# Transposing the last 64 keys of a mixed attention tile: one fp32 matmul with 128 weight columns from a zero-padded tile, in place of two with 64

## The chip, the cores and the metric

The kernel runs on one core of a Trainium2 chip, in one launch. The metric is device time in microseconds (us). A core has TensorE (PE in the profile, with its weight loads as PEld), VectorE (DVE), ScalarE (ACT), GpSimd (POOL) and SyncE (SP, which issues most DMAs). Each engine works through its own list in order and waits on semaphores where it needs another's result.

## What is computed

Four batches of 576 tokens go through attention with 8 heads of 64, then a gated expert layer, then a Fourier mixing layer with an MLP. The change lies in the attention, which keeps only scores close to each row's largest:

```python
scores = scale * np.matmul(q, k.transpose(0, 1, 3, 2))
thresh = np.max(scores, axis=-1, keepdims=True) - tau
scores = np.where(scores >= thresh, scores, -1000000000.0)
scores = scores - np.max(scores, axis=-1, keepdims=True)
attn = np.exp(scores)
attn = attn / (np.sum(attn, axis=-1, keepdims=True) + 1e-09)
return np.matmul(attn, v)
```

Behind it stand two matrix products with a squared ReLU between them and a sigmoid gate (the expert layer), and then the two Fourier transforms, a normalisation and two more products (the mixer).

## The kernel before, in words

**Tiles.** The 32 heads are worked on as 16 pairs (`pi`), two heads (`j` = 0, 1) each. A head has 576 = 4 x 128 + 64 query rows, so a pair has eight tiles of 128 rows that belong to one head, and a ninth, the *mixed* tile, with the last 64 rows of head 0 on partitions 0 to 63 and those of head 1 on partitions 64 to 127. The nine are the steps of a pair, the mixed one the fifth. Step `n` of the whole program is `9 * pi + s`.

**One step.** PE makes the scores of a tile from a query tile and the keys, which are split into a high and a low part (`kh`, `kl`) so that two fast matmuls give fp32 accuracy (L212, and L226 for the mixed tile). DVE takes the row maximum (L252), ACT the exponential (L263), DVE drops what lies below the threshold and sums (L267), takes the reciprocal (L626, L630), and `emit_norm` multiplies the tile by it (L273 on POOL; in the first four pairs most tiles on ACT, L636). The tile `e` is then transposed on PE, 128 keys at a time, since the product with V needs keys on partitions. ACT and DVE split each transpose into a high and a low part (L305, L306). Eight or so of these feed `emit_av` (L387, L389).

**The last 64 keys.** 576 keys are four blocks of 128 and 64 more. A head's own tiles get the 64 along with 64 of the other head (L340). In the mixed tile both heads' last 64 keys stand in columns 512 to 575, on different partitions, and the product with V wants head 0's keys on partitions 0 to 63 and head 1's on 64 to 127. `emit_Tmix` therefore ends, in `out2`, with two matmuls (L365): weights are all 128 rows and 64 columns of `e`, the moving operand is a set of 32 identity columns that picks one head's half, and each writes one half of the partitions of `t2`:

```python
for j in range(2):
    c = 64 * j + 32 * half
    pe.matmul(t2[64 * j:64 * j + 64], e[:, 512:576], ident[:, c:c + 32], start=True, stop=True)
```

They are fp32 and not transposes. `emit_Tmix` runs twice for each pair (`half` = 0, 1), so there are 32 places in the program and 64 such matmuls. Four whole transposes of the mixed tile stand ahead of each place (L353).

**Stages.** In the first four pairs only attention runs, while DVE, ACT and POOL also split the expert weights (`weight_pieces`, L54 to L73: L67 to L69 on DVE, L72 on ACT, L73 on POOL). From the fifth pair on, the expert layer of the batches that are done runs between the attention's steps (`ffn_stream`: L413 to L415, and L523 to L525, three matmuls for each product). The mixer comes last.

**What sets the order.** The program is written step by step, with a priority for each kind of work (`hp`), and a scheduler puts each engine's instructions in order from its own estimates, so an edit at one place can move rows at others. A tile of the pool `at` with one buffer (`em`, the raw head loads `raw`) is written again only when its last reader is done. A raw load is released when the splits (L151 on POOL, L167 on DVE) have read it.

Of the kernel before, what the change touches and what calls it, by code (L numbers as in the profile page):

```python
# [9 lines left out]
F32 = mybir.dt.float32  # L10
F32R = mybir.dt.float32r
I32 = mybir.dt.int32
ALU = mybir.AluOpType
AF = mybir.ActivationFunctionType
# [7 lines left out]
NPAIR = H // 2  # L22
# [6 lines left out]
def tile_kernel(ctx: ExitStack, tc: tile.TileContext, a):  # L29
    nc = tc.nc  # L30
    pe, dve, act, pool, sp = nc.tensor, nc.vector, nc.scalar, nc.gpsimd, nc.sync
# [8 lines left out]
    ident = const.tile([128, 128], F32, name="ident")  # L40
# [54 lines left out]
    at = astack.enter_context(tc.tile_pool(name="at", bufs=1, side="right"))  # L95
# [42 lines left out]
    heads, vts, ptu, ptr, et, em, sps, stat, xT = ({} for _ in range(9))  # L138
# [7 lines left out]
    def conv_k(pi, j):  # L146
        raw = heads[pi, j][0]
        kh = at.tile([128, S], F32R, tag="kh", bufs=3, name="kh")
        kl = at.tile([128, S], F32R, tag="kl", bufs=3, name="kl")
        act.activation(kh, raw[:, 640:], AF.Copy)  # L150
        (dve if pi + j == 0 else pool).tensor_tensor(kl, raw[:, 640:], kh.bitcast(F32), op=ALU.subtract)  # L151
        heads[pi, j] += [kh, kl]
# [19 lines left out]
    vtile = at.tile([128, 10, 128], F32R, name="v")  # L172
    pool.memset(vtile[:, 8:10].bitcast(F32), 0.0)

    def load_v(pi):
        b, pr = divmod(pi, NPAIR)
        raw = at.tile([128, 9, DH], F32, tag="raw", name="rawv")
        sp.dma_start(raw, a["v"][b, pr])
        vts[pi] = raw
# [14 lines left out]
    def step_of(n):  # L194
        pi, s = divmod(n, 9)
        return pi, ORDER[s]
# [34 lines left out]
    def eview(n):  # L231
        pi, tl = step_of(n)
        if tl is None:
            if n not in em:
                em[n] = at.tile([128, S], F32, tag="em", name="em")
            return em[n]
        j, i = tl
        if (pi, i) not in et:
            m = 4 * pi + i
            if P['E3'] and m % 3 == 2 and m < 4 * NPAIR - 2:  # L240
                et[pi, i] = stage.tile([128, 2 * S], F32, tag="e", name="e3")
            else:
                et[pi, i] = at.tile([128, 2 * S], F32, tag="e", bufs=2, name="e")
        return et[pi, i][:, j * S:(j + 1) * S]
# [23 lines left out]
            e, sps[n][:, :, 0:HS], st[:, 1:2], e, op0=ALU.is_ge, op1=ALU.mult, accum_out=st[:, 2:3]  # L268
        )

    def emit_norm(n):
        st, e = stat[n], eview(n)
        pool.tensor_scalar(e, e, st[:, 2:3], 1.0, op0=ALU.mult, op1=ALU.mult)  # L273

    def emit_front(n):

# [72 lines left out]
    def emit_Tmix(pi, half):  # L349
        e = em[pi * 9 + 4]  # L350
        t = pst.tile([128, 4, 2, 2, 32], F32, tag="t", name="tm")
        for k in range(4):
            pe.transpose(t[:, k].rearrange("p a b c -> p (a b c)"), e[:, 128 * k:128 * (k + 1)], ident)  # L353
        sl = slice(256, HS)

        def out():
            for j in range(2):
                u = unit(pi, j, half)
                split_out(u[:, 0, :, sl], u[:, 1, :, sl], t[:, :, j, half, :])

        def out2():
            t2 = pst.tile([128, 32], F32, tag="t", name="tm2")
            for j in range(2):
                c = 64 * j + 32 * half
                pe.matmul(t2[64 * j:64 * j + 64], e[:, 512:576], ident[:, c:c + 32], start=True, stop=True)  # L365
            r = rem_unit(pi, half)
            split_out(r[:, 0, sl], r[:, 1, sl], t2)

        return [out, out2]
# [200 lines left out]
    sp.dma_start(mus[:, 0:4], a["mu_k"])  # L570
    sp.dma_start(mus[:, 4:8], a["mu_r"])
    dve.tensor_scalar(mus[:, 8:16], mus[:, 0:8], -1.0, 1.0, op0=ALU.mult, op1=ALU.add)
    conv_k(0, 1)
    conv_q(0, 1)
    load_v(0)
    conv_v(0)

# [31 lines left out]
    def do_front(n, pi, s):  # L609
        cur = 0 <= n < NSTEP  # L610
        nxt = range(state['m'], min(n + ahead(n), NSTEP - 1) + 1)
        state['m'] = max(state['m'], n + ahead(n) + 1)
        k = 1
        if s != 4 and P['SM' if pi >= NPAIR else 'SM0'] >> ((s - (s > 4)) // 2) & 1:

            k = 0 if s in (0, 2, 5, 7) else 2
        g = stats.rearrange("p (s c) -> p s c", c=3)[:, s + 1 - k:s + 1]
        with hp('pF'):
            if cur:
                emit_select(n)  # L620
        with hp('pM'):
            for m in nxt:
                emit_max(m)
        with hp('pF'):
            if cur and k:
                dve.tensor_scalar(g[:, :, 2], g[:, :, 2], 1e-9, None, op0=ALU.add)  # L626
            for m in nxt:
                emit_th(m)
            if cur and k:
                dve.reciprocal(g[:, :, 2], g[:, :, 2])  # L630
        with hp('pN'):
            for m in range(n + 1 - k, n + 1):
                if cur:
                    if P['NA' if pi >= NPAIR else 'NA0'] >> (m % 9) & 1:
                        e = eview(m)
                        act.activation(e, e, AF.Copy, scale=stat[m][:, 2:3])  # L636
                    else:
                        emit_norm(m)

    def do_av(n, pi, s):  # L640
        for d in range(2):
# [74 lines left out]
    for n in range(NSTEP + 8):  # L716
        pi, s = divmod(n, 9)
# [347 lines left out]
    for (q, g), f in mixer():  # L1065
# [4 lines left out]
        if f == 2 and (q, g) in ahead_of:  # L1070
            while (q, g) == (0, 5) and not fft_done:
                next(behind)
            n = ahead_of[q, g]
# [134 lines left out]
```

## Time and profile before

| what | value |
|---|---|
| median of 3 runs | 1136.56 us (1135.72 to 1139.6) |
| the profiled execution | 1139.89 us, of which 1138.1 us is the span of the trace |
| busy, share of the span | PE 91%, PEld 84%, DVE 71%, ACT 52%, POOL 43% |
| mean granted TensorE clock | 0.969 of full speed |
| instructions | 19981, on PE 7109 matmuls |
| DMA | 114.07 MB, mean 100 GB/s |

The busy shares are means over stages with different limits, so the rows further down are taken stage by stage. A matmul's end in the profile is modelled; its start is not, so PE is read by the distance between starts. In a form like `128*64 128x32` the first is the weights' rows and columns and the second the moving operand's.

### The profile page before, as it was taken

The page shows a single profiled execution, that of the slowest core. Times are in us where ns is not written, and L with a number is a line of the kernel's source. Part 1 is how long each engine was busy: PE and PEld are TensorE (multiplying, and loading weights), DVE is VectorE, ACT ScalarE, POOL GpSimd, SP SyncE. Part 2 cuts the span into 40 slices and gives each one's busy share as a digit, 9 for nine tenths or more (in the row PEclk, how much of TensorE's full clock was granted, in tenths as well). Part 3 has the DMA queues.
Part 4 walks back from the last instruction along what each step waited for, and adds up shares of the span by engine and source line. Part 5 has one row for each costly group of instructions (what it writes and reads, how often), then busy time and mean ns, then how long its engine had stood idle before and what let it go on. Part 6 is the DMA issues. An engine that isn't in the chain of part 4 may idle for free.

```text
span 1138.1 us, 19981 instructions
## 1 busy us (share of the span) xinstructions
PE 1038.4 (91%) x7109; PEld 960.0 (84%) x7109; DVE 806.7 (71%) x2093; ACT 588.9 (52%) x1396; POOL 483.8 (43%) x633
## 2 busy tenths in 40 slices
PE   4566769999999999999999997999999999999998
PEld 3555649999988999889988986889999999999997
DVE  7999889889889798897865677975553959322222
ACT  5787777768586685866736564433331212111111
POOL 4556576746467364673634253530001636100000
PEclk9888789999999999999999998999999999999999
DMA  5333321101112011121016255663442546223231
GB/s 171 111 119 96 98 73 56 48 30 54 55 56 76 30 47 56 56 76 32 24 65 159 93 162 178 199 205 120 153 143 90 185 158 190 98 93 109 77 111 56
DMA packets 40395, 114.07 MB, mean 100 GB/s; under 512 B 6191, under 2 KB 6612, under 8 KB 40296
## 3 DMA queue, kind: packets, MB, share of 16 engines
q1 hardware_dynamic: 27200, 74.57, 20.4%
q0 software_dynamic: 10400, 33.50, 9.1%
q10 hardware_dynamic: 2696, 4.73, 1.2%
q8 instruction: 56, 0.92, 0.3%
q14 instruction: 43, 0.35, 0.1%
HBM read 84.45 MB, written 28.32 MB: 99 GB/s over the span
## 4 chain that ended last, share of the span: by engine, by line
PE 65%; DVE 16%; ACT 7%; DMA 6%; issue 4%; POOL 2%; SPq 0%; DVEq 0%; ACTq 0%; POOLq 0%
PE c1ps L969 6%; PE c1ps L971 6%; PE c1ps L970 6%; PE c2ps L984 6%; PE c2ps L982 6%; PE c2ps L983 6%; PE av L387 3%; PE s L212 3%; DVE q L167 3%; DMA rawqk<-in_qk 2%; PE t L320 2%; DVE small L252 2%; PE kps L413 2%; DVE e L267 2%; PE kps L415 2%
## 5 line engine op out<-in xcount | busy, mean ns | idle before, releaser
L975 DVE SCALAR_TENSOR_TENSOR hl<-c1ps,hh 128x256 fp32r<-128x256 f32 x144 | 60.4, 421 | 161.2 <-ACT hh L974 160.6
L974 ACT ACTIVATE hh<-c1ps 128x256 fp32r<-128x256 f32 x144 | 54.3, 379 | 205.7 <-PE c1ps L971 205.6
L252 DVE TENSOR_REDUCE small<-s 128x1 f32<-128x576 f32 x144 | 107.3, 750 | 15.7 <-PE s L212 14.7
L1007 POOL DMA_DIRECT2D ud<-u x54 | 29.5, 546 | 194.2 <-DVE u L1006 138.4
L267 DVE SCALAR_TENSOR_TENSOR e<-s,small,e 128x576 f32<-128x576 f32 x128 | 102.4, 811 | 7.3 <-ACT e L263 5.6
L273 POOL TENSOR_SCALAR e<-e,small 128x576 f32<-128x576 f32 x104 | 82.3, 797 | 46.4 <-DVE small L630 35.4
L263 ACT ACTIVATE e<-s,small 128x576 f32<-128x576 f32 x128 | 92.6, 742 | 14.4 <-DVE small L252 13.4
L212 PE MATMUL s<-kh,q 128*128 128x288 f32 x256 | 65.4, 340 | 29.8 <-DVE q L167 13.7
L320 PE MATMUL t<-ident,e 128*128 128x128 f32 x512 | 81.2, 290 | 7.9 <-DVE ptr L306 2.9
L969 PE MATMUL c1ps<-ut,cA 128*128 128x256 f32 x288 | 82.5, 286 | 2.2 <-ACT ut L960 1.5
L970 PE MATMUL c1ps<-ut,cA 128*128 128x256 f32 x288 | 82.0, 285 | 0.0
L523 PE MATMUL vps<-k,wv 128*128 128x288 f32 x256 | 76.7, 302 | 5.4 <-DVE tg L529 4.6
L971 PE MATMUL c1ps<-ut,cA 128*128 128x256 f32 x288 | 81.6, 283 | 0.0
L971 PE MATMUL c1ps<-ut,cB 128*128 128x256 f32 x288 | 81.0, 281 | 0.0
L969 PE MATMUL c1ps<-ut,cB 128*128 128x256 f32 x288 | 80.9, 281 | 0.0
L970 PE MATMUL c1ps<-ut,cB 128*128 128x256 f32 x288 | 80.7, 280 | 0.0
L485 POOL TENSOR_TENSOR k<-relu,k 128x288 fp32r<-128x288 f32 x64 | 54.1, 847 | 60.6 <-ACT k L483 59.7
L306 DVE TENSOR_TENSOR pt<-t,pt 128x512 fp32r<-128x512 f32 x100 | 67.8, 684 | 16.4 <-ACT pt L305 15.7
L413 PE MATMUL kps<-xh,wk 128*128 128x288 f32 x256 | 78.3, 306 | 0.8 <-ACT relu L470 0.4
L387 PE MATMUL av<-pt,v 128*128 128x288 f32 x408 | 71.3, 308 | 8.1 <-ACT pt L305 3.8
L414 PE MATMUL kps<-xl,wk 128*128 128x288 f32 x256 | 75.8, 296 | 0.0
L415 PE MATMUL kps<-xh,wk 128*128 128x288 f32 x256 | 75.6, 296 | 0.0
(240 smaller groups left out, 3552.8 us busy)
## 6 DMA issues: line engine op xcount, KB each, us to landing
rawqk<-in_qk SPq DMA_DIRECT2D x32, 608.0 KB
u<-ud SPq DMA_DIRECT2D x36, 512.0 KB
wraw<-in_w_ch POOLq DMA_DIRECT2D x64, 256.0 KB, 3.3
ud<-u POOLq DMA_DIRECT2D x54, 256.0 KB, 2.5
rawv<-in_v SPq DMA_DIRECT2D x16, 288.0 KB
un<-ud SPq DMA_DIRECT2D x18, 256.0 KB
out<-u SPq DMA_DIRECT2D x18, 256.0 KB
wraw<-in_w_k SPq DMA_DIRECT2D x8, 512.0 KB
```

The lines of the kernel that those rows point to most:

```text
L212: pe.matmul(ps[:, h, 0:HS], q[:, c:c + 128], kk[:, h * HS:(h + 1) * HS], start=(x == 0), stop=(x == 1),)
L252: dve.tensor_reduce(st[:, 0:1], sps[n][:, :, 0:HS], axis=AX.XY, op=ALU.max, negate=True)
L263: act.activation(two(eview(n)), sps[n][:, :, 0:HS], AF.Exp, bias=st[:, 0:1])
L267: dve.scalar_tensor_tensor(e, sps[n][:, :, 0:HS], st[:, 1:2], e, op0=ALU.is_ge, op1=ALU.mult, accum_out=st[:, 2:3])
L273: pool.tensor_scalar(e, e, st[:, 2:3], 1.0, op0=ALU.mult, op1=ALU.mult)
L320: pe.transpose(t[:, k, :], e[:, o + 128 * k:o + 128 * (k + 1)], ident)
L387: pe.matmul(ps, v[:, 4 * j + k, :], u[:, x, k, :], start=(k == 0 and x == 0), stop=False)
L413: pe.matmul(ps, wh, x[0][:, k, :], start=(k == 0), stop=False)
L415: pe.matmul(ps, wl, x[0][:, k, :], start=False, stop=(k == nk - 1))
L969: pe.matmul(ps, wh, ut[0][:, k, :], start=(k == 0), stop=False)
L970: pe.matmul(ps, wh, ut[1][:, k, :], start=False, stop=False)
L971: pe.matmul(ps, wl, ut[0][:, k, :], start=False, stop=(k == 3))
```

## The change

A tile `ez` of 128 x 128 is zeroed once at the start. The norm of a mixed tile is now three instructions: columns 0 to 511 in place as before, and columns 512 to 575 of each head's 64 rows into `ez`, head 0's into the upper left quarter and head 1's into the lower right one. A second tile `icomb` holds the sum of the two halves of the identity. One matmul with `ez` as weights, 128 columns wide, and 32 columns of `icomb` then gives both heads' halves at once. The choice between ACT and POOL moves into `emit_norm` and stays as it was.

```diff
--- before.py
+++ after.py
@@ -171,6 +171,11 @@
 
     vtile = at.tile([128, 10, 128], F32R, name="v")
     pool.memset(vtile[:, 8:10].bitcast(F32), 0.0)
+
+
+    ez = at.tile([128, 128], F32, name="ez")
+    pool.memset(ez, 0.0)
+    icomb = at.tile([128, 64], F32, name="icomb")
 
     def load_v(pi):
         b, pr = divmod(pi, NPAIR)
@@ -268,9 +273,19 @@
             e, sps[n][:, :, 0:HS], st[:, 1:2], e, op0=ALU.is_ge, op1=ALU.mult, accum_out=st[:, 2:3]
         )
 
-    def emit_norm(n):
+    def emit_norm(n, on_act=False):
         st, e = stat[n], eview(n)
-        pool.tensor_scalar(e, e, st[:, 2:3], 1.0, op0=ALU.mult, op1=ALU.mult)
+        parts = [(e, e, slice(0, 128))]
+        if step_of(n)[1] is None:
+            parts = [(e[:, 0:512], e[:, 0:512], slice(0, 128))]
+            for j in range(2):
+                r = slice(64 * j, 64 * j + 64)
+                parts.append((ez[r, r], e[r, 512:576], r))
+        for o, i, r in parts:
+            if on_act:
+                act.activation(o, i, AF.Copy, scale=st[r, 2:3])
+            else:
+                pool.tensor_scalar(o, i, st[r, 2:3], 1.0, op0=ALU.mult, op1=ALU.mult)
 
     def emit_front(n):
 
@@ -360,9 +375,7 @@
 
         def out2():
             t2 = pst.tile([128, 32], F32, tag="t", name="tm2")
-            for j in range(2):
-                c = 64 * j + 32 * half
-                pe.matmul(t2[64 * j:64 * j + 64], e[:, 512:576], ident[:, c:c + 32], start=True, stop=True)
+            pe.matmul(t2, ez, icomb[:, 32 * half:32 * half + 32], start=True, stop=True)
             r = rem_unit(pi, half)
             split_out(r[:, 0, sl], r[:, 1, sl], t2)
 
@@ -570,6 +583,7 @@
     sp.dma_start(mus[:, 0:4], a["mu_k"])
     sp.dma_start(mus[:, 4:8], a["mu_r"])
     dve.tensor_scalar(mus[:, 8:16], mus[:, 0:8], -1.0, 1.0, op0=ALU.mult, op1=ALU.add)
+    dve.tensor_tensor(icomb, ident[:, 0:64], ident[:, 64:128], op=ALU.add)
     conv_k(0, 1)
     conv_q(0, 1)
     load_v(0)
@@ -631,11 +645,7 @@
         with hp('pN'):
             for m in range(n + 1 - k, n + 1):
                 if cur:
-                    if P['NA' if pi >= NPAIR else 'NA0'] >> (m % 9) & 1:
-                        e = eview(m)
-                        act.activation(e, e, AF.Copy, scale=stat[m][:, 2:3])
-                    else:
-                        emit_norm(m)
+                    emit_norm(m, P['NA' if pi >= NPAIR else 'NA0'] >> (m % 9) & 1)
 
     def do_av(n, pi, s):
         for d in range(2):
```

Line numbers move by 5 to 14 in the changed kernel (L365 is L378 there, L523 to L525 are L536 to L538, L273 and L636 are L288 and L286). Three places show how the order on the engines moves.

PE, second stage, at the place that stands at 503 us in the trace of the kernel before (`vps` is the expert layer's second product, `tm` the result of the transpose). Before:

```order
L523 MATMUL vps<-k_5695,wv_86 128x288
L524 MATMUL vps<-k_5696,wv_86 128x288
L525 MATMUL vps<-k_5695,wv_87 128x288
L365 MATMUL tm_6285<-ident,em 64x32 x2
L523 MATMUL vps<-k_5695,wv_86 128x288
L524 MATMUL vps<-k_5696,wv_86 128x288
L525 MATMUL vps<-k_5695,wv_87 128x288
L212 MATMUL s<-kh,q 128x288 x2
```

With the change:

```order
L536 MATMUL vps<-k_5701,wv_86 128x288
L537 MATMUL vps<-k_5702,wv_86 128x288
L538 MATMUL vps<-k_5701,wv_87 128x288
L378 MATMUL tm_6291<-icomb,ez 128x32
L536 MATMUL vps<-k_5701,wv_86 128x288
L537 MATMUL vps<-k_5702,wv_86 128x288
L538 MATMUL vps<-k_5701,wv_87 128x288
L217 MATMUL s<-kh,q 128x288 x2
```

The neighbours are the same; two matmuls with 64 columns have become one with 128.

POOL, second stage, around the norm of the same pair's mixed tile (`kl` is the key split that releases a raw head load). Before:

```order
L189 TENSOR_TENSOR v<-rawv,v 128x4x64
L189 TENSOR_TENSOR v<-rawv,v 64x64
L273 TENSOR_SCALAR em<-em,small 128x576
L273 TENSOR_SCALAR e<-e,small 128x576
L151 TENSOR_TENSOR kl<-rawqk,kh 128x576
L441 TENSOR_TENSOR xl<-xtmp,xh 128x288 x2
L273 TENSOR_SCALAR e<-e,small 128x576
```

With the change:

```order
L194 TENSOR_TENSOR v<-rawv,v 128x4x64
L194 TENSOR_TENSOR v<-rawv,v 64x64
L288 TENSOR_SCALAR em<-em,small 128x512
L288 TENSOR_SCALAR ez<-em,small 64x64 x2
L288 TENSOR_SCALAR e<-e,small 128x576
L151 TENSOR_TENSOR kl<-rawqk,kh 128x576
L454 TENSOR_TENSOR xl<-xtmp,xh 128x288 x2
L288 TENSOR_SCALAR e<-e,small 128x576
```

The two small multiplies stand between the mixed tile's norm and the next tile's, and the key split comes behind them.

ACT, first stage, around the fourth pair's mixed tile (140 us in the trace). Before:

```order
L72 ACTIVATE wv_86<-wbits 128x512
L395 ACTIVATE xt<-avs 64x288
L188 ACTIVATE v<-rawv 64x64
L305 ACTIVATE ptr<-t_1307 128x128
L636 ACTIVATE em<-em,small 128x576
L331 ACTIVATE e<-t 128x512
L332 ACTIVATE pt<-t 128x4x128
L263 ACTIVATE e<-s,small 128x576 x2
```

With the change:

```order
L193 ACTIVATE v<-rawv 128x4x64
L320 ACTIVATE ptr<-t_1311 128x128
L193 ACTIVATE v<-rawv 64x64
L408 ACTIVATE xt<-avs 64x288
L286 ACTIVATE em<-em,small 128x512
L286 ACTIVATE ez<-em,small 64x64 x2
L408 ACTIVATE xt<-avs 64x288
L193 ACTIVATE v<-rawv 64x64
L346 ACTIVATE e<-t 128x512
```

The three norm instructions stand together; two copies of attention results (`xt`) and the parts of `v` have other places around them.

## Rows read from the trace of the kernel before

**Rows 1.** Page, part 2: granted TensorE clock in tenths, 40 slices of 28.45 us.

```profile
PEclk9888789999999999999999998999999999999999
```

**Rows 2.** Windows view, two stretches (length, then busy us and instructions by engine, clock, DMA).

```profile
0.00:184.00 184.00, 116.29 (x633) 101.86 (x634) 163.09 (x410) 134.17 (x275) 112.84 (x108) 0.84 0.35 107
184.00:590.00 406.00, 390.25 (x2982) 375.08 (x2982) 345.47 (x970) 284.62 (x676) 230.85 (x306) 1.00 0.15 47
```

**Rows 3.** Line view of L365, whole run: ns min/median/max of weight loads and matmuls.

```profile
L365 PEld LDWEIGHTS tm<-ident,em x128: 132/136/232, 41.6 to 584.7; 128*64 128x64 f32 x128
L365 PE MATMUL tm<-ident,em x128: 222/243/316, 41.6 to 584.7; 128*64 128x32 f32 x128
```

**Rows 4.** Timeline of PE matmuls, 502.9 to 504.4 us (start, length, what).

```profile
503.03 0.29 PE L525 MATMUL vps<-k,wv 128*128 128x288 f32 x1
503.25 0.31 PE L365 MATMUL tm<-ident,em 128*64 128x32 f32 x4
503.49 0.40 PE L523 MATMUL vps<-k,wv 128*128 128x288 f32 x1
503.73 0.29 PE L524 MATMUL vps<-k,wv 128*128 128x288 f32 x1
503.86 0.29 PE L525 MATMUL vps<-k,wv 128*128 128x288 f32 x1
```

**Rows 5.** Timeline of PE weight loads, same stretch.

```profile
502.90 0.19 PEld L525 LDWEIGHTS vps<-k,wv 128*128 128x128 f32 x1
503.25 0.20 PEld L365 LDWEIGHTS tm<-ident,em 128*64 128x64 f32 x4 [0.17 <-DVE small L626]
```

**Rows 6.** Timeline of PE matmuls around four full-width fp32 transposes, 582.3 to 583.3 us.

```profile
582.37 0.30 PE L525 MATMUL vps<-k,wv 128*128 128x288 f32 x1
582.50 0.60 PE L353 MATMUL tm<-ident,em 128*128 128x128 f32 x4
582.85 0.38 PE L523 MATMUL vps<-k,wv 128*128 128x288 f32 x1
583.07 0.30 PE L524 MATMUL vps<-k,wv 128*128 128x288 f32 x1
```

**Rows 7.** Timeline of PE matmuls around one with 33 rows, 623.0 to 623.9 us.

```profile
623.03 0.28 PE L817 MATMUL fa<-tc,G 128*128 128x258 f32 x1
623.24 0.38 PE L818 MATMUL fa<-talt,g 33*128 33x258 f32 x1
623.55 0.39 PE L824 MATMUL fb<-ts,H 128*128 128x256 f32 x1
```

**Rows 8.** Groups of POOL by line and shape (count, busy us, mean ns, idle before).

```profile
L437 POOL TENSOR_SCALAR xtmp<-xt,small 128x288 f32<-128x288 f32 x64 | 35.1, 554 | 28.4 <-DVE xl L441 15.3 <-DVE xt L396 12.3
...
L273 POOL TENSOR_SCALAR em<-em,small 128x576 f32<-128x576 f32 x12 | 9.0, 749 | 16.0 <-DVE small L630 9.0 <-DVE small L259 7.0
```

**Rows 9.** Groups of ACT by line and shape.

```profile
L188 ACT ACTIVATE v<-rawv 64x64 fp32r<-64x64 f32 x32 | 7.9, 248 | 0.4
...
L636 ACT ACTIVATE em<-em,small 128x576 f32<-128x576 f32 x4 | 3.1, 764 | 0.0
```

**Rows 10.** Chain of waits, 0 to 300 us (start, length, what).

```profile
2.58 3.07 DMA small<-in_mu_r
...
140.30 0.66 ACT em L636
```

**Rows 11.** Timeline of POOL, 497.5 to 500.7 us.

```profile
497.77 0.75 POOL L273 TENSOR_SCALAR em<-em,small 128x576 f32<-128x576 f32 x1 [3.52 <-DVE small L259]
...
499.21 1.43 POOL L151 TENSOR_TENSOR kl<-rawqk,kh 128x576 fp32r<-128x576 f32 x1
```

**Rows 12.** Chain of waits, 184 to 590 us.

```profile
499.65 1.69 DVE q L167
501.39 3.79 DMA rawqk<-in_qk
```

**Rows 13.** Groups of DVE by line and shape: one step of the weight conversion.

```profile
L68 DVE SCALAR_TENSOR_TENSOR wbits<-wraw,wbits 128x512 int32<-128x512 int32 x20 | 19.7, 986 | 0.1
```

## Prediction

> **What bounds the kernel now.** Read the granted clock first. In the first 184 us it moves between the two levels (1.2 and 2.4 GHz); from then on it stands at full speed but for one dip [rows 1]. The windows view shows two different stages in the part that the change touches [rows 2]. From 0 to 184 us PE is busy for 116.29 us and DVE for 163.09: DVE sets the pace, and a shorter PE step is worth little. From 184 to 590 us, where the other twelve pairs' attention runs between the matmuls of the first expert layer, PE is busy for 390.25 of 406.00 us at full clock. Its idle time is 15.75 us, 4%: work taken off PE here should shorten the stage. After 590 us no mixed tile is left, since the last L365 record starts at 584.7 us [rows 3]. Next read what one pair of L365 matmuls costs there, by start times, because the profile models the ends of matmuls.
>
> The 128 records are two passes for each of the 64 fp32 matmuls, so each of the 32 places in the program has four [rows 3]. In [rows 4], ordinary 288-column matmuls start 0.13 us apart. L525 starts at 503.03, the four records at 503.25, the next L523 at 503.49 and the one behind it at 503.73: 0.70 us, where two ordinary steps would take 0.27. **The place costs 0.43 us.** It is not computing for all of it. The loads show why: the load for L525 starts at 502.90, 0.13 us ahead of its own matmul, but the first 64-column load starts only at 503.25 [rows 5], with its own matmul and 0.22 us behind the last [rows 4]. A load that should lie under the matmul before it does not. On the way out it takes 0.24 us from one start to the next, twice.
>
> Is that fp32, or the half-width array? Two neighbours tell. Four fp32 transposes with 128 weight columns run from 582.37 to 583.07, also 0.70 us, so four cost 0.43 and one 0.11 us, with no gap around them [rows 6]. An ordinary-type matmul that uses only 33 rows at a partition offset has the gaps: 0.21 us ahead of it and 0.31 behind [rows 7], against the 0.13 of [rows 4]. So the gaps go with the part of the array, not with fp32.
>
> **The change part by part.**
>
> *PE.* Each place loses two matmuls (four loads of 64 columns) and gets one with 128 columns (two passes, two loads). No row shows a full-width fp32 matmul that is not a transpose, so I bound it. Lower: two passes at the transposes' 0.11 us, no gaps, 0.22 us [rows 6]: 0.43 - 0.22 = 0.21 us saved. Upper: the gaps stay, because the two passes of fp32 cause them. Then the two loads, one behind the other, take the place of four that overlapped. The four records last 0.31 us together and one matmul at least 0.222, so their starts lie within 0.09 us [rows 3, 4]; two loads 0.11 apart cost 0.02 more, or 0.13 more if each pass takes its whole 0.11. I take the lower end: [rows 7] has the gaps without fp32 and [rows 6] has fp32 without gaps. Of the 96 records in the stage, 24 places x 0.215 = **5.2 us less**. The eight early places count as nothing, since DVE is ahead there; at half clock each could save 0.43, 3.4 us in all, and I keep that for the lower end of the range.
>
> *POOL.* For twelve of the sixteen mixed tiles, one 576-column multiply becomes three. From 288 to 576 columns it goes from 554 to 749 ns [rows 8], 0.68 ns a column: 512 columns make 0.71 us and each 64-column one some 0.40. So 1.50 in place of 0.75: 0.75 us more, 9.0 in all, and at least nothing if the small ones were free. POOL is idle for 175 of the 406 us [rows 2]. What stands behind it matters: in [rows 11] the mixed multiply, the next tile's, and then the split of the keys into kl follow back to back. That kl ends at 500.64. The next load into the same raw buffer starts at 501.39, and in the chain it waits for DVE's q, which ends at 501.34 [rows 12]. So 0.70 us of the 0.75 is covered, and I count zero. Without that cover it is the third rival.
>
> *ACT.* Four mixed tiles are scaled on ACT: 764 ns becomes some 0.71 for 512 columns and two small ones of at least 248 ns each [rows 9], with the scale read from a tensor perhaps 0.34: +0.45 to +0.62 us. In the chain of the first stage one of the four stands [rows 10]. I count one, **0.6 us more**; none to four makes 0 to 2.5.
>
> *DVE and the start.* The sum of the two identity halves stands ahead of the 1 - mu step, for which the chain waits until 5.65 us anyhow [rows 10]: zero. If the identity landed last it would be one small operation. Zeroing ez is one memset before POOL has work: zero.
>
> *Waits.* The norm writes ez where it wrote em's last columns, and reads its place before the next pair's norm; em already had that wait, and earlier (the exponential). Nothing new is waited for. The 512-column multiply ends a little sooner, the 64-column part later, and two steps lie between them and the transposes.
>
> *The order.* The scheduler has put many things elsewhere in the first stage. The PE rows around the mixed tiles later are nearly the same. Where a weight conversion of three DVE operations of about 1 us [rows 13] comes ahead of or behind what the chain needs, a place like that is worth up to 3 us either way; I take zero.
>
> *Sum.* -5.2 on PE; a tenth of it, 0.6, is lost because the chain through q and the raw loads [rows 12] becomes last in places; +0.6 on ACT: **-4.0 us**. The profiled execution took 1139.89 us (span 1138.1 and 1.8 around it), so 1135.9 for it; the median of the runs is 1136.56, 3.3 below, so **1132.6 us**.
>
> **The rivals.**
>
> *1. The gain is taken by other waits.* PE is shortened, but the head loads and q (3.79 and 1.69 us in the chain [rows 12]) keep the pairs' rhythm. For it: they recur in the chain. Against: PE idles only 4%. Then -5.2 leaves -1 or nothing: 1135 to 1137.
>
> *2. The gaps stay.* By the upper bound 24 x 0.02 to 0.13 = 0.5 to 3.1, and 0.6 on ACT: 1137.7 to 1140.3. For it: no row has this form. Against: [rows 6, 7]. The Trainium skill speaks for it with another reason (TensorEngine Tiling (Array Packing), Key Properties): different tiles of the array can load weights and multiply in parallel, so the merge gives up a concurrency. The overlap in [rows 5], four loads in 0.20 us, agrees with that page; by it alone the sum would be this rival's.
>
> *3. POOL becomes last: slower.* At the mixed tile, kl comes late by 0.75 us, the raw buffer comes free late, and the next head's load, q and scores follow. It decides where the small multiplies cost over 0.35 us each, since the cover is 0.70 us. Wholly on the path: +9.0 - 5.2 + 0.6 = +4.4, 1141.0. For it: 0.40 is beyond 0.35. Against: q on DVE would have to end no later than now, and only 0.05 us a pair lies open.
>
> *4. The order outweighs the rest*: one or two conversions that move ahead of or behind the chain in the first stage, 3 to 6 us either way on top of the forecast: 1126.6 to 1129.6, or 1135.6 to 1138.6.
>
> **How the numbers follow.** A measurement of this kernel tells about 0.3%, 3.4 us, from no change. Forecast 60% (1127 to 1135: of these 41 are below 1133.2 and 19 within), rival 1 10% (within), rival 2 10% (7 within, 3 slower), rival 3 12% (slower), rival 4 8% (4 faster, 2 within, 2 slower). Faster 0.45, same 0.38, slower 0.17. The range goes from 1126.5 (5.2, with the early 3.4 and some luck of order) to 1140.3, the end of rival 2; beyond it lie rival 3 and the tails.
>
> **What would show it.** L365's line becomes 64 records with 128 weight columns. Right: the next ordinary matmul but one starts 0.49 us after the one ahead of the pair, not 0.70, and its first load starts with the matmul before it; the 24 places end the stage about 5 us earlier, with PE's idle time near 16 us. Wrong: a gap still ahead of that load (rival 2); PE idle time grown by about 5 us behind q (rival 1) or behind kl, with POOL's small multiplies above 0.35 us (rival 3); a first stage that is several us longer or shorter (rival 4).

## The result and the profile after

The changed kernel takes **1152.01 us** (median of 4 runs, 1149.51 to 1152.84); the kernel before, run beside it on the same chip, 1137.39. The ratio is 1.0118 with a 95% interval of 1.0101 to 1.0135: slower by 1.2%, where 1132.6 us and a gain of 0.35% were forecast. The profiled execution took 1149.51 us (span 1147.7) against 1139.89 (1138.1).

The part of the change that the argument rested on did what it was to do. The line view of L378 (the new matmul) answers to [rows 3], and the timelines of PE matmuls and weight loads at the same place of the program answer to [rows 4, 5]:

```profile
L378 PEld LDWEIGHTS tm<-icomb,ez x64: 186/190/338, 41.2 to 593.8; 128*128 128x128 f32 x64
L378 PE MATMUL tm<-icomb,ez x64: 190/275/422, 41.2 to 593.9; 128*128 128x32 f32 x64
```

```profile
509.94 0.29 PE L538 MATMUL vps<-k,wv 128*128 128x288 f32 x1
510.07 0.30 PE L378 MATMUL tm<-icomb,ez 128*128 128x32 f32 x2
510.21 0.38 PE L536 MATMUL vps<-k,wv 128*128 128x288 f32 x1
510.43 0.29 PE L537 MATMUL vps<-k,wv 128*128 128x288 f32 x1
```

```profile
509.81 0.19 PEld L538 LDWEIGHTS vps<-k,wv 128*128 128x128 f32 x1
509.94 0.32 PEld L378 LDWEIGHTS tm<-icomb,ez 128*128 128x128 f32 x2
```

From L538 to the second matmul behind the pair it is now 0.49 us (509.94 to 510.43), in place of 0.70 in [rows 4]. The median of the stage's 24 places is the same, 0.70 before and 0.49 now. The first load starts with the matmul ahead of it (509.94), where in [rows 5] it started 0.22 us behind. The gap went with the half-width weights. The Trainium skill says that a change of tiling mode makes TensorE drain (TensorEngine Tiling (Array Packing), Key Properties: "Mode switching requires drain"). The 0.22 us ahead of a 64-column load, and their absence here, agree with that.

The windows view answers to [rows 2]:

```profile
0.00:184.00 184.00, 117.67 (x614) 103.62 (x615) 161.61 (x410) 136.90 (x284) 114.47 (x113) 0.77 0.35 107
184.00:590.00 406.00, 382.25 (x2874) 369.45 (x2873) 340.30 (x955) 280.67 (x665) 237.52 (x324) 1.00 0.15 47
```

The first stage has a lower granted clock (0.77, before 0.84) and ends when it did; DVE is busy for 161.61 of its 184 us. In the middle stage PE is busy for 382.25 us of the 406 in place of 390.25, yet the stage is longer: the last record of the mixed tiles starts at 593.9 us and not at 584.7 [rows 3], while the first k projection (L413, L426 in the changed kernel), which begins the stage, starts at 174.4 against 174.6. From one to the other it is 419.5 us in place of 410.1. So nearly the whole loss, 9.4 of 9.6 us, arises between these two points. PE's own waits there show what it is made of. The view of waits of PE, first for the kernel before (175 to 585 us), then for the changed one (174 to 594 us); columns: who waited for whom, total us, times, longest (`tg` is the second product of the expert layer times its gate):

```profile
PE av L387 <- ACT pt L305: 3.8, 5, 1.2
PE vps L523 <- DVE tg L529: 2.8, 2, 1.4
PE t L340 <- DVE pt L306: 2.4, 5, 0.9
...
PE s L212 <- DVE e L267: 0.5, 2, 0.3
...
PE tm L353 <- DVE pt L306: 0.3, 1, 0.3
```

```profile
PE t L355 <- DVE pt L321: 5.1, 8, 1.3
PE s L217 <- DVE e L272: 3.5, 6, 1.4
PE tm L368 <- DVE pt L321: 3.0, 3, 1.5
PE av L400 <- ACT pt L320: 2.6, 3, 1.2
PE vps L536 <- DVE tg L542: 2.4, 2, 1.7
```

All rows of the first view add up to 15.3 us, those of the second to 25.0. Three of them, transposes and scores that wait for DVE, make 8.4 of the 9.7 us more (11.6 in place of 3.2). TensorE's saving is there, 0.21 us at each of 24 places, which I take as the 5.2 us of the forecast, and waits of 9.7 us stand against it. The third item is the clock: one stretch of 3.4 us, at 185.7 us, runs at the lower level, which costs at most half of that, 1.7 us. A stretch so short does not show in a row like [rows 1]: the slice around it still reads 9. That makes -5.2 + 9.7 + 1.7 = +6.2 of the 9.4. The other 3.2 us are not idle time: PE is idle for 15.7 us of the 410.1 before and for 25.3 of the 419.5 after, which is about what the two views add up to. They lie in stretches in which PE counts as busy, and no row shows them singly.

Last, the norm. Groups of POOL and ACT by line and shape answer to [rows 8, 9]:

```profile
L288 POOL TENSOR_SCALAR em<-em,small 128x512 f32<-128x512 f32 x12 | 8.4, 700 | 15.6 <-DVE small L644 11.9 <-DVE small L264 3.5
L288 POOL TENSOR_SCALAR ez<-em,small 64x64 f32<-64x64 f32 x24 | 7.6, 318 | 1.1
...
L286 ACT ACTIVATE ez<-em,small 64x64 f32<-64x64 f32 x8 | 2.7, 339 | 0.1
```

A small multiply takes 318 ns on POOL (estimated: 400) and 339 on ACT (estimated: 340).

### The profile page after: what moved, and what is told of

The parts are those of the page before. It is cut to its first block, busy times and chain, and to the rows that moved or that the text cites. A ratio compares the mean times of both kernels' runs of the same rounds, so it can differ in the third digit from the quotient of the medians.

```text
span 1147.7 us, 19898 instructions
## 1 busy us (share of the span) xinstructions
PE 1041.1 (91%) x7045; PEld 964.9 (84%) x7045; DVE 810.4 (71%) x2094; ACT 590.9 (51%) x1404; POOL 494.0 (43%) x658
## 4 chain that ended last, share of the span: by engine, by line
PE 62%; DVE 18%; ACT 8%; DMA 6%; issue 4%; POOL 2%; SPq 0%; DVEq 0%; ACTq 0%; POOLq 0%
PE c1ps L979 5%; PE c1ps L981 5%; PE c2ps L994 5%; PE c2ps L992 5%; PE c2ps L993 5%; PE c1ps L980 5%; PE av L400 3%; DVE q L167 3%; PE s L217 3%; DMA rawqk<-in_qk 3%; PE t L335 3%; PE vps L536 2%; DVE small L257 2%; PE kps L426 2%; PE vps L537 2%
## 5 line engine op out<-in xcount | busy, mean ns | idle before, releaser
L288 POOL TENSOR_SCALAR e<-e,small 128x576 f32<-128x576 f32 x104 | 84.4, 817 | 56.5 <-DVE small L644 47.3
L217 PE MATMUL s<-kh,q 128*128 128x288 f32 x256 | 66.8, 346 | 34.3 <-DVE q L167 15.7
L536 PE MATMUL vps<-k,wv 128*128 128x288 f32 x256 | 76.7, 302 | 3.7 <-DVE tg L542 2.8
L426 PE MATMUL kps<-xh,wk 128*128 128x288 f32 x256 | 78.8, 308 | 1.0 <-DVE xt L409 0.5
L335 PEld LDWEIGHTS t<-ident,e 128*128 128x128 f32 x512 | 64.3, 148 | 17.8 <-DVE ptr L321 6.0
L217 PEld LDWEIGHTS s<-kh,q 128*128 128x128 f32 x256 | 45.0, 213 | 40.6 <-DVE q L167 16.3
```

The source lines that it names most:

```text
L217: pe.matmul(ps[:, h, 0:HS], q[:, c:c + 128], kk[:, h * HS:(h + 1) * HS], start=(x == 0), stop=(x == 1),)
L288: pool.tensor_scalar(o, i, st[r, 2:3], 1.0, op0=ALU.mult, op1=ALU.mult)
L335: pe.transpose(t[:, k, :], e[:, o + 128 * k:o + 128 * (k + 1)], ident)
L426: pe.matmul(ps, wh, x[0][:, k, :], start=(k == 0), stop=False)
L536: pe.matmul(ps, wv[0][:, c:c + 128], k2[0][:, k, :], start=(k == 0), stop=False)
```

## The experiments

To take the change apart without the scheduler moving anything else, most kernels below carry a table of the order in which each engine's instructions stand, and chain them in it; the chain adds no wait on another engine. "Old order" is that of the kernel before, "new order" that of the changed one; an instruction that only one of them has stands next to its neighbours there. No kernel has the old work chained in the old order alone, so what the chain itself costs is not measured; experiments 4 and 8, each with the old order and one edit, stand at 0.9999 and 1.0008. "Matmul alone" (4 and 9) leaves the last 64 keys of the mixed tiles out of the result.

```diff
         astack.close()
...
+    keep_order(tc)
```

| kernel | us (median) | before | ratio, 95% interval |
|---|---|---|---|
| 1. new work, old order | 1142.66 | 1138.98 | 1.0033 (1.0021 to 1.0045) |
| 2. old work, new order | 1149.90 | 1138.98 | 1.0100 (1.0083 to 1.0117) |
| 3. split norm alone, old order | 1144.96 | 1138.98 | 1.0056 (1.0042 to 1.0070) |
| 4. matmul alone, old order | 1139.09 | 1139.18 | 0.9999 (0.9988 to 1.0010) |
| 5. new work, old order, multiplies in idle places | 1140.07 | 1139.18 | 1.0011 (0.9996 to 1.0026) |
| 6. as 5, most multiplies on DVE | 1140.61 | 1139.18 | 1.0013 (0.9998 to 1.0028) |
| 7. new work, new order to 174 us only | 1142.75 | 1139.18 | 1.0032 (1.0017 to 1.0048) |
| 8. before, load in two parts | 1139.75 | 1138.44 | 1.0008 (0.9993 to 1.0024) |
| 9. as 4, load in two parts | 1135.97 | 1138.44 | 0.9977 (0.9965 to 0.9988) |
| **10. as 5, load in two parts** | **1136.11** | 1138.44 | **0.9972 (0.9961 to 0.9983)** |
| 11. before, small matmuls four times | 1148.30 | 1138.44 | 1.0081 (1.0068 to 1.0094) |
| 12. new work, new order from 174 us | 1152.47 | 1138.45 | 1.0126 (1.0106 to 1.0145) |
| 13. changed kernel, load in two parts | 1146.13 | 1138.45 | 1.0062 (1.0047 to 1.0077) |
| 14. as 1, load in two parts | 1137.63 | 1138.45 | 0.9994 (0.9983 to 1.0005) |
| 15. as 6, load in two parts | 1140.52 | 1138.45 | 1.0017 (1.0007 to 1.0027) |
| 16. old work, new order to 314 us | 1145.36 | 1138.79 | 1.0061 (1.0042 to 1.0080) |
| 17. old work, new order from 314 us | 1147.12 | 1138.79 | 1.0071 (1.0053 to 1.0089) |

### 1 to 3: order, and split norm

> The changed kernel's instructions, held engine by engine in the order of the kernel before; the pair of 64-column matmuls is one 128-column matmul in its place and the three multiplies stand where the one stood. Order theory (the scheduler's new order costs some 18 us, the work itself saves 4): about 1133 us, 4 below the kernel before. Multiply theory (the small multiplies on POOL and ACT cost it, wherever they stand): about 1152. If the matmul itself costs it in some way that its starts do not show: also about 1152.

> The kernel before, instruction for instruction, held in the order that the changed kernel has. Order theory: 1152 and the 4 us of the work that is not saved, 1154 to 1157 us. Multiply theory and matmul theory: 1137, as the kernel before, since the order costs nothing.

> The kernel before with only the mixed tile's norm cut in three (512 columns and two pieces of 64 rows by 64, in place), in the order of the kernel before; both 64-column matmuls stay. Order theory: within 2 us of the kernel before, since POOL is covered and one ACT norm of four counts with 0.6 us. Multiply theory: 1152 to 1157. Matmul theory: 1137.

The edit of the third, in the norm of the mixed tile of the kernel before:

```diff
-        pool.tensor_scalar(e, e, st[:, 2:3], 1.0, op0=ALU.mult, op1=ALU.mult)
+            parts = [(e[:, 0:512], slice(0, 128))]
+            for j in range(2):
+                r = slice(64 * j, 64 * j + 64)
+                parts.append((e[r, 512:576], r))
```

None of the three came out at a time that I had set down: each theory has a part of it. The order alone costs 1.00%, the new work alone 0.33%, and together they make about the 1.18% of the changed kernel. The split norm alone costs 0.56%. So both terms that the prediction put at nothing are wrong, and the order is the larger. The waits of PE in the second kernel (172 to 596 us) name the same culprits as the changed kernel, with none of its work:

```profile
PE t L340 <- DVE pt L306: 5.1, 7, 1.3
PE s L212 <- DVE e L267: 3.1, 5, 1.7
PE tm L353 <- DVE pt L306: 3.0, 3, 1.5
```

### 4, 11: what TensorE's time is worth

> The changed kernel's matmul with zeros and its combined identity, in the order of the kernel before, but with the norm of the mixed tile left as one instruction over 576 columns: nothing is written behind the zeros, so the last 64 keys of the mixed tiles are left out of the result. This is the matmul part of the change by itself. Theory: the whole 5.2 us that TensorE saves reach the end and the first two experiments lost them again to the split norm, then this runs at 1133.8 us (before 1139.0). Rival: the parts simply add up, so that all new work in the old order (+3.7) less the split norm alone (+6.0) leaves 2.3 us for the matmul, then 1136.7 us. If TensorE's time did not matter at all it would be 1139.

```diff
+        if on_act:
+            act.activation(e, e, AF.Copy, scale=st[:, 2:3])
+        else:
+            pool.tensor_scalar(e, e, st[:, 2:3], 1.0, op0=ALU.mult, op1=ALU.mult)
```

> The kernel before, in its own order, with the two small matmuls of each of the 32 places issued four times over (the last two overwrite with the same values), so TensorE has work added in place of taken away. By the trace of before a further pass took 0.01 to 0.07 us, so 12 further ones add 0.3 us a place, 7 us over the 24 places of the middle stage. If TensorE sets that stage: 1144 to 1147 us. If it has waits there that take it up, as it has to if taking work away changed nothing: 1139 to 1142 us.

```diff
-            for j in range(2):
+            for j in (0, 1) * 4:
```

Taking the 5.2 us away changes nothing (0.9999); adding time costs most of it or all. In experiment 11 one place grew by 0.34 us, from 0.70 to 1.04, and 24 of them make 8.2 us; the kernel became 9.2 us slower (0.0081 x 1138.44; by the interval 7.7 to 10.7). In the one execution with a trace the middle stage grew by 6.2 us (416.3 in place of 410.1), and PE's waits in it shrank from 15.3 to 13.0. Timeline of PE there:

```profile
509.63 0.29 PE L525 MATMUL vps<-k,wv 128*128 128x288 f32 x1
509.85 0.66 PE L365 MATMUL tm<-ident,em 128*64 128x32 f32 x16
510.44 0.40 PE L523 MATMUL vps<-k,wv 128*128 128x288 f32 x1
510.67 0.30 PE L524 MATMUL vps<-k,wv 128*128 128x288 f32 x1
```

So waits took up a part of the added time at most, and the bolder reading that TensorE does not set this stage fell. It does, but other things are close behind it. Where a part of the saving goes can be seen at one place. Timelines of PE, the kernel before, then matmul alone:

```profile
323.90 0.29 PE L415 MATMUL kps<-xh,wk 128*128 128x288 f32 x1
324.41 0.50 PE L212 MATMUL s<-kh,q 128*128 128x288 f32 x2 [0.21 <-DVE e L267]
```

```profile
323.21 0.29 PE L421 MATMUL kps<-xh,wk 128*128 128x288 f32 x1
323.94 0.49 PE L217 MATMUL s<-kh,q 128*128 128x288 f32 x2 [0.43 <-DVE e L272]
```

Just behind the mixed tile the scores wait for DVE's selection: 0.21 us before, 0.43 now. The 0.22 us won is waited away within 1 us. Where no such wait stood, the lead lasted until PE caught up with DVE somewhere else: at the vps matmuls near 367 us PE waited for 1.81 us from start to start before, 2.76 us now.

The clock cost something too in this execution, as the windows view shows, in the kernel before and then in matmul alone (the granted clock is the third column from the end: 1.00 and 0.52 in the second rows):

```profile
366.00:368.00 2.00, 0.57 (x5) 0.54 (x5) 1.97 (x6) 1.04 (x3) 2.00 (x3) 1.00 0.41 126
368.00:370.00 2.00, 2.00 (x17) 2.00 (x17) 2.00 (x6) 0.78 (x2) 1.30 (x3) 1.00 0.06 22
```

```profile
366.00:368.00 2.00, 0.34 (x2) 0.34 (x3) 1.97 (x5) 0.84 (x3) 2.00 (x3) 1.00 0.31 69
368.00:370.00 2.00, 2.00 (x11) 2.00 (x10) 2.00 (x6) 0.99 (x3) 1.50 (x3) 0.52 0.23 87
```

After the longer idle time the granted clock fell to the lower level, and 2 us held 11 matmuls in place of 17. Not every such wait did that: in experiment 5 the same place waited for 2.9 us from start to start, at full clock.

The same execution has a second stretch of 3.4 us at the lower level, at 272.5 us, where no idle time of PE just ahead is over 1 us. Its window, and timelines of PE at its two ends, the kernel before and then matmul alone:

```profile
272.50:275.90 3.40, 3.40 (x16) 3.40 (x15) 2.64 (x10) 2.65 (x8) 2.91 (x5) 0.50 0.21 77
```

```profile
272.23 1.06 PE L320 MATMUL t<-ident,e 128*128 128x128 f32 x8 [0.95 <-DVE pt L306]
...
275.61 0.50 PE L212 MATMUL s<-kh,q 128*128 128x288 f32 x2
```

```profile
271.49 1.07 PE L328 MATMUL t<-ident,e 128*128 128x128 f32 x8 [0.97 <-DVE pt L314]
...
276.40 0.52 PE L217 MATMUL s<-kh,q 128*128 128x288 f32 x2
```

A lead of 0.74 us becomes a lag of 0.79. The two stretches cost some 1.5 us each, 3.0 us together, and PE's waits add up to 2.9 us more than before (18.2 and 15.3): in this execution the clock takes as much of the saving as the waits do. The kernel before has no such stretch between the first k projection and the last mixed tile of its trace.

### 5, 6: where the small multiplies stand

> All the work of the changed kernel in the old order, as in the experiment with the new work in the old order (1142.7 us), with one difference: the two small multiplies of a mixed tile no longer stand right behind the norm, but on the same engines (POOL in 12 tiles, ACT in 4) at a place where the trace of the kernel before shows that engine idle between the norm and the matmul, in 6 of the 12 POOL tiles behind kl. Theory (the small multiplies push POOL's kl into DVE's q, which then takes up to twice as long, and DVE is late from there on): kl starts as early as before, the loss goes and the matmul's gain is left, 1135 to 1138 us. Rival (any extra 0.64 us on POOL costs, wherever it stands): 1142 to 1143.

POOL's order at one mixed tile:

```diff
 em<-em,small
-ez<-em,small
-ez<-em,small
 e<-e,small
 kl<-rawqk,kh
+ez<-em,small
+ez<-em,small
 xl<-xtmp,xh
```

> As the experiment before this one, but in 13 of the 16 mixed tiles the two small multiplies become one DVE instruction over 128 columns (the 64 columns read twice, times the scale, times a tile of ones and zeros), at a place where DVE is idle in the trace of the kernel before by 0.2 to 1.1 us; in the other three they stay on ACT (2) and POOL (1). Estimate 0.2 to 0.3 us for one. Theory (DVE waits there for a matmul or a load anyway, and POOL has no more to do than before): 1134 to 1137 us. Rival (DVE is the bound and pays each one in full, 13 x 0.25 = 3.3 us): 1137 to 1141.

```diff
+            dve.scalar_tensor_tensor(ez.rearrange("p (a b) -> p a b", a=2), x, st[:, 2:3], mask.rearrange("p (a b) -> p a b", a=2), op0=ALU.mult, op1=ALU.mult)
```

The place is worth 2.6 us (1142.66 to 1140.07; ratios 1.0033 and 1.0011, with intervals that touch), and experiment 5 lies between the two times that were expected. Timelines of POOL, and of DVE's q, for new work in the old order, then for experiment 5; [rows 11, 12] have the kernel before:

```profile
500.58 0.73 POOL L288 TENSOR_SCALAR ez<-em,small 64x64 f32<-64x64 f32 x2
501.40 0.75 POOL L288 TENSOR_SCALAR e<-e,small 128x576 f32<-128x576 f32 x1
502.12 2.00 POOL L151 TENSOR_TENSOR kl<-rawqk,kh 128x576 fp32r<-128x576 f32 x1
...
501.82 1.01 DVE L167 SCALAR_TENSOR_TENSOR q<-rawqk,small,q 64x640 fp32r<-64x640 f32 x1 [0.37 <-ACT q L157]
```

```profile
500.44 1.43 POOL L152 TENSOR_TENSOR kl<-rawqk,kh 128x576 fp32r<-128x576 f32 x1
501.85 1.29 POOL L298 TENSOR_SCALAR ez<-em,small 64x64 f32<-64x64 f32 x2
...
500.87 1.68 DVE L168 SCALAR_TENSOR_TENSOR q<-rawqk,small,q 64x640 fp32r<-64x640 f32 x1 [0.29 <-ACT q L158]
```

Before, kl starts first (499.21), takes 1.43 us, and q beside it 1.69: q ends last, and the next load follows it. With 0.73 us of multiplies ahead, kl starts 0.30 us behind q. Now q takes 1.01 us and **kl 2.00**, and the chain of waits has changed hands:

```profile
502.15 1.98 POOL kl L151
504.14 3.75 DMA rawqk<-in_qk
```

That is the place of rival 3. The cover of 0.70 us did not hold, because kl did not keep its 1.43 us. But it happens in few places: of the 24 heads from the 9th on, kl is the last reader of none before and in experiment 5, of 2 in experiment 1 (by 1.31 and 1.30 us, together as much as experiment 5 gives back), of 3 in the changed kernel (together 3.8 us), one of which the old work in the new order has too. The reason written ahead of experiment 5, that q takes longer and DVE is late, is not what the trace shows: q of these 24 heads sums to 32.3 us before and 32.1 in experiment 1. What is late is the load.

On DVE the multiplies are neither better nor worse (1.0013 and 1.0011), inside the range of the rival written ahead of experiment 6.

### 7, 12, 16, 17: where the order costs

> All the work of the changed kernel, in the new order up to the first k projection (about 174 us) and in the old order from there on. If the cost of the order lies behind the first k projection, as the delay of the changed kernel against the one before suggests (0 at 174 us, 4 at 250 us), this runs like the new work in the old order, 1142 to 1144 us. If it lies in the first 174 us, it runs like the changed kernel, 1150 to 1153 us.

> The mirror image of the experiment with the new order in the first stage alone: all work of the changed kernel, in the old order up to the first k projection (about 174 us) and in the new order from there on. If the order's cost lies in the middle stage and later, this runs like the changed kernel less what little the first stage took, 1149 to 1152 us. If both halves are needed for the loss, 1143 to 1147.

> The work of the kernel before, in the new order up to the 77th row maximum of DVE (314 us in the trace of before) and in the old order from there on; in the new order all through it took 1.0 % longer. In the trace of that run the delay against the kernel before grows from nothing at 174 us to some 4 us at 290, stands still to 500, and grows by 4 to 7 more from 500 to 560. If this split is right, here only the first part is paid: 1142 to 1144 us. If the early delay is made up for later whatever the order, 1138 to 1140.

> The reverse: the work of the kernel before, old order up to 314 us and new order from there on. By the same trace the later part is 4 to 7 us: 1142 to 1146 us. If the loss is one that adds up evenly over the places, the two parts come to about the same, 5.5 us each; if the parts do not add up to 11 us together, some of the loss needs both.

The edit of these is the table alone: one order up to the cut, the other behind it. The first stage, where the new order looked most different, is worth nothing: 1.0032 with its new order, 1.0033 with the old. All of the cost lies behind the first k projection (1.0126), and it is spread: 0.61% up to 314 us and 0.71% from there, both some 1 us above what was expected. Their sum of 1.32% is over the 1.00% of the whole, which only the lower ends of the intervals (0.42 and 0.53) reach. No single place explains it, and which of the moved instructions does it stays open. The clock may have a part: in the trace of experiment 2 two stretches of 3.4 us in the middle stage run at the lower level (183 and 518 us), in that of 16 one and in that of 17 none.

### 8 to 10, 13 to 15: the chain behind TensorE

In the kernel before, a head's keys and queries and a pair's values pass through one raw buffer. DVE's q is its last reader, and the next load waits for it [rows 12]. The edit makes two buffers of the same total size, so that the load of keys need not wait for q, and queries don't wait for kh:

```diff
-        raw = at.tile([128, 1216], F32, tag="raw", name="rawqk")
-        sp.dma_start(raw, a["qk"][b, pr, j])
+        raw = at.tile([128, S], F32, tag="rawk", name="rawk"), at.tile([128, 640], F32, tag="rawq", name="rawq")
+        sp.dma_start(raw[0], a["qk"][b, pr, j][:, 640:])
+        sp.dma_start(raw[1], a["qk"][b, pr, j][:, 0:640])
...
-        raw = at.tile([128, 9, DH], F32, tag="raw", name="rawv")
+        raw = at.tile([128, 9, DH], F32, tag="rawk", name="rawv")
```

> The kernel before, in its own order, with one change that has nothing to do with the mixed tile: the buffer into which the raw keys and queries of a head, and the raw values, are loaded one after the other (608 KB and 288 KB) becomes two, one for keys and values and one for queries, of the same total size, and the load becomes two loads. Theory: the middle stage is set by the loop load of rawqk (3.8 us), ACT's kh (0.69) and q (0.73), DVE's q (0.9 to 1.7), next load of rawqk, and not by TensorE; then a loop whose query part needs no kh before it and is half as long a load gives back 1 to 1.5 us in each of the 12 later pairs: 1121 to 1130 us. Rival (TensorE sets the middle stage, as the prediction had it): 1137 to 1140, no change.

> The matmul alone (the last 64 keys of the mixed tiles left out of the result, as in that experiment) with the load in two parts. Theory: the 5.2 us of TensorE did not reach the end because the load loop set the pace; with the loop loosened 3 to 5 us of it pass, so this is 0.3 to 0.5 % below the kernel before with the split load. Rival (DVE's own work sets the pace behind the loop): the same time as the kernel before with the split load, within 1 us.

> All work of the changed kernel, old order, the small multiplies at places where their engine was idle, with the load in two parts. If the loop was what the small multiplies hurt (they delayed kl and with it the next load), this is at or below the kernel before with the split load, and by 0.5 to 1.5 % below the kernel before: a version that beats both. Rival (the small multiplies cost by themselves): 1 to 4 us above the kernel before with the split load.

> The changed kernel in its own order, with the load of keys and queries in two parts and nothing else. Theory: in the new order TensorE waits for DVE at more places (21 to 25 us of waits in the middle stage in place of 15), and few of these waits hang on the load, so the split gives back no more than it did in the old order, 2 to 6 us: 1146 to 1150. Rival (the new order hurts because it puts the work of the load loop later): most of the 11 us comes back, 1139 to 1143.

> All work of the changed kernel in the old order with the small multiplies right behind the norm (1142.7 us with the single load), and the load in two parts. Against the experiment with all work, the multiplies in idle places and the split load (1136.1) it tells what the place of the multiplies is worth once the loop is loosened. Theory (the multiplies push kl into DVE's q, which then takes longer, whatever the load does): 1138 to 1141. Rival (they only hurt by way of the loop): 1135 to 1137.

> The small multiplies as one DVE instruction in 13 tiles, at places where DVE was idle, with the load in two parts. With the single load this was level with the multiplies on POOL at idle places (1140.6 to 1140.1). Theory: level again, 1135 to 1138. If DVE's own work has become the bound behind the loop, its 13 instructions show in full, 13 x 0.25 = 3 us: 1138 to 1140.

Alone, the split load gives nothing (1.0008), a clear miss of the 9 to 18 us that I expected; alone, the matmul gives nothing (0.9999). Together they give 0.23% against the kernel before and 0.31% against the split load alone (0.9977 over 1.0008), 3.5 us, as two chains of about the same length would. That reading is not shown, because it has a rival in the traces. Between the first k projection and the last mixed tile experiment 9 takes 407.9 us and experiment 4 takes 411.8, and 3.0 of these 3.9 us are the two stretches at the lower clock in experiment 4; experiment 9 has none. Whether the other executions are like these two is not known: the mean granted clock of a whole execution, 0.963 in experiment 4 and 0.960 in experiment 9 on average, moves with the first stage too. With the multiplies in idle places it is a whole kernel again that is a little faster than the kernel before and than the changed one: **0.9972**, 1136.11 us, short of the 0.5 to 1.5% that was expected.

The split load is no cure for the order: the changed kernel falls from 1.0118 to 1.0062, but the same work in the old order falls from 1.0033 to 0.9994, so the order still costs 0.68%. The place of the multiplies goes on to matter: right behind the norm 0.9994, in idle places 0.9972. And on DVE they now cost 0.45% more than on POOL (1.0017 and 0.9972), which they didn't with the single load. DVE's own work as a third chain would do that, but no trace shows it as the cause, and the trace of experiment 15 has a stretch at the lower clock (510 us) that experiment 10 lacks. The groups of DVE in experiment 15, and the line view of the same line:

```profile
L296 DVE SCALAR_TENSOR_TENSOR ez<-em,small,mask 128x128 f32<-128x128 f32 x13 | 10.1, 775 | 0.0
```

```profile
L296 DVE SCALAR_TENSOR_TENSOR ez<-em,small,mask x13: 340/647/1514, 104.8 to 570.1; 128x128 f32<-128x128 f32 x13
```

I had estimated 0.25 us for one; the mean is 0.775.

## Why the prediction was wrong, step by step

- **PE, 24 places x 0.215 us: right** on the engine, to the hundredth (0.70 to 0.49 us). Rival 2, that the gaps stay, is out.
- **"Work taken off PE here should shorten the stage": wrong.** An engine that is busy for 390 of 406 us need not be alone at the limit. Added work costs most of its time or all (experiment 11), removed work gives nothing (4), and it gives 3.5 us once the load is in two parts (9 against 8). The prediction lost a tenth of the 5.2 us to waits and nothing to the clock; in the trace of experiment 4, waits take 2.9 us more and the clock 3.0. The sum reads the stage's full clock from [rows 1, 2] and gives it no term. Rival 1 (the gain is taken by other waits) has the time that came for the matmul alone, 1135 to 1137 us, and a part of the mechanism.
- **POOL, "0.70 us of the 0.75 is covered, and I count zero": wrong.** The small multiplies were cheaper than estimated (0.32 and not 0.40), but the cover was worked out with a kl of 1.43 us. Behind q it takes 2.00. Rival 3 has the right place, but a deciding point set too high (0.35 us each) and the wrong count: kl became last at two tiles of twelve. The split norm alone costs 0.56%, of which the trace shows one such tile (1.29 us) and one stretch of 3.4 us at the lower clock (514 us); the rest is not told apart.
- **ACT, +0.6 us: not seen, and too small to be seen.** The first k projection starts at 174.4 us, 0.2 earlier than before, though the multiplies took what was estimated. In the traces of the experiments that start lies anywhere from 171.7 to 176.7 us.
- **The order, "I take zero": the step that failed most.** I gave rival 4 8% and looked for it in the first stage. It costs 1.00% by itself, all of it behind that stage, where I had written that the rows around the mixed tiles are nearly the same. At the place shown they are. In the whole middle stage they are not: of the 3015 matmul records of PE there, at most 2635 stand in the same order in experiment 2, and of DVE's 989 instructions 797. It shows as 8 us more in three kinds of waits for DVE.
- **The range** allowed one rival at a time. Order (+1.0%) and new work (+0.33%) came together, and the second was itself a loss in place of -4.0 us.

What stays open: which moves of the order cost; how much of what experiments 4 and 9 show is the load chain and how much the clock; and why the matmul's saving, worth nothing by itself, is worth 0.23% beside the split norm (0.56% without it, 0.33% with it).

## What to carry to other kernels

Before a saving on a busy engine is counted, look for the chain that is as long as it: ask what the next wait behind the place hangs on, and test it by adding work as well as by taking it away. When two traces are compared, look for short stretches at the lower clock in each: one or two of them can hide a saving of this size. Where a scheduler sets the order, a small edit can cost more by what it moves elsewhere than by what it does; keep the old order as one version, or the two can't be told apart. And a cover worked out from durations holds only as long as the order of the covered instructions stays what it was.

## What was not expected of the hardware

- **DVE's q and POOL's kl beside each other:** the one that starts first keeps its length or nearly, the other stretches. q takes 0.88 us alone and 1.68 behind kl; kl takes 1.43 us ahead of q and 2.00 behind it. The Trainium skill has this for a DVE instruction with two inputs in SBUF and a GpSimd instruction that reads SBUF (SBUF — State Buffer, SBUF: two separate sides): an exclusive lock on a shared port pair, which whichever starts first gets "for the whole instruction". The direction agrees; fully blocked, kl would have ended at 501.82 + 1.01 + 1.43 = 504.26 us, and it ended at 504.12. The prediction used the two durations without it.
- **One DVE operation on 128 x 128 with a mask** took between 0.34 and 1.51 us. The longest stand just behind kl, as in experiment 15 (timelines of POOL and of DVE); at nearly the same place of experiment 6 kl is not beside it, and it took 0.34 us:

```profile
356.08 1.43 POOL L153 TENSOR_TENSOR kl<-rawk,kh 128x576 fp32r<-128x576 f32 x1
...
356.14 1.51 DVE L296 SCALAR_TENSOR_TENSOR ez<-em,small,mask 128x128 f32<-128x128 f32 x1
```

- **A wait of PE can cost twice:** the wait near 367 us in experiment 4 was followed by a stretch at the lower clock, at 0.24 us a matmul in place of 0.13, that cost 1.5 us more: the kernel was 0.2 us behind the one before at the first of these matmuls and 1.7 at DVE's tg behind them. The stretch at 272.5 us cost as much with no idle time over 1 us just ahead of it, so the length of one wait does not tell here whether the clock falls.
